# Linear attention and a gated network on one core: one list chooses the next instruction for every queue, and the first batch's norms come from products with ones

## The chip, the cores and the metric

The kernel runs on one core of a Trainium2 chip. The metric is device time in microseconds (us), from the start of one execution to its end. The five queues of the core work side by side and in order: PE (TensorE, matrix products; weight loads are shown apart as PEld), DVE (VectorE), ACT (ScalarE), POOL (GpSimd) and SP (SyncE, which here only issues transfers). An instruction that waits holds up all that stand behind it on its queue.

## The reference

Random-feature attention of 8 batches, 8 heads, 576 tokens and head dimension 64 feeds a gated network:

```
proj = x @ omega.T                   # omega 128 x 64, for q and k, scaled by 64 ** -0.25
h    = proj - sum(x * x) / 2;  phi = exp(h - max(h)) / sqrt(128)
kv   = k_p.T @ v;  z = sum over tokens of k_p
x    = (q_p @ kv) / (q_p @ z + 1e-6)         # 4608 tokens x 512
y    = sigmoid(x @ w_gate) * (x @ w_val)      # 4608 x 1536
out  = y @ w_out                              # 4608 x 512
```

Everything is float32. The network's weights come as 64-bit floats and are converted on the chip.

## The kernel before

**Stages.** The kernel has three stretches on TensorE. The first makes attention, and between its products those of the *first pass* of the network: gate and value of the first 4 of 12 column tiles of the hidden layer (tile `gv`). The second makes the other hidden columns (`gw`), the third the output (`po`). Of the first pass, 18 products are kept back and run between attention and the second stretch. The second and third stretch are written in a fixed order, which the change leaves alone; between attention and the second stretch it changes only at which products the weights `u` are loaded and split.

**Attention.** Two batches make a unit `u` (4 of them), with 9 tiles of 128 tokens and 4 pairs of heads `p`. A unit has two halves `b`; keys and queries of each half are tasks of their own, for each pair of heads (`keys` and `queries`, lines 780 to 883). A task loads its input (`rawk`, `rawq`, loaded at the top of `projected`, line 714), splits it in a high part (`hik`, `hiq`, on ACT) and a low part (`lok`, `loq`, on POOL), multiplies both with omega in three products (`ppk`, `ppq`), takes maxima on DVE, and goes on: keys to an exponential on ACT (`kpk`) and the product with v (`pkv`), queries to a subtraction (`hq`, DVE), transposes (`ptq`), an exponential (`qpq`, ACT), a product with `kv` (`pnq`), a division (`denq`, `invq`, `xq`, DVE), transposes (`pxq`), and a copy on ACT (`xsq`, 2 buffers) that goes to `xT` in memory. The first pass reads `xT` back (`xr`), splits it on ACT and POOL (`xe`) and multiplies.

**Norms.** The sums of squares come from a second copy of the input with tokens on partitions (`natk`, `natq`): for each half of a unit and of keys or queries, `norms` (line 686) loads 4 or 5 tiles of 128 x 512, squares them on ACT (`x2k`, `x2q`) and sums over each head on DVE (`ssk`, `ssq`). A task's first product with omega is not put down before its norms are.

**Weights.** `conversions` (line 284) is one long chain of 18 units `c`, each of two halves: two loads, six DVE instructions and one on POOL per half (`from_float64`, line 177), then for the first 4 units a split into `wh` and `wl`, which the first pass multiplies with, and for the others sums on POOL and a store `w32`. The load of the next unit is issued a unit ahead.

**Who orders the work.** The order of PE, DVE, ACT and POOL in attention is settled while the kernel is built. `Clock` (line 76) keeps an account of when each engine would be free and each tile written; `attention` (line 917) asks it and chooses the next step. In the kernel before, TensorE's account is "now": steps of other engines are put down while their engine is at most 2 us ahead, conversions when DVE has room, first-pass products when no attention product is due, and a hook, `filler`, slips DVE steps of conversions into attention's DVE steps. Transfers have no queue in the account: one lands 2.5 us after it could start. The account gives every float32 product 230 columns' time, and does not know TensorE's two clock levels. SP is not among the engines with an order of their own; its transfers follow the program text.

```
        if engine == "PE" and ins[0].dtype == F32:
            n = self.FULL
...
            self.written[o] = max(self.at["PE"], after, self.used.get(o, 0.0)) + self.DMA
```

Of the kernel before, what the change touches and what calls it, by code (L numbers as in the profile page):

```python
# [18 lines left out]
DM = H * D  # L19
DF = 1536  # L20
P = 128
# [27 lines left out]
LEFT = 18  # L49
SMALL = 16  # L50
SQS = 6
MARGIN = 0.5
QUEUED = 2.0
CONV_QUEUED = 0.0
CONV_LATE = 1.2
CONV_END = 0.97
CONV_FILL = 1.0
# [3 lines left out]
RAWS, SPLITS, KPS, VS, HS, XS = 6, 6, 6, 3, 4, 4  # L61
# [14 lines left out]
class Clock:  # L76
# [6 lines left out]
    DMA = 2.5  # L83
    FULL = 230

    def __init__(self):
        self.at = dict.fromkeys(self.COST, 0.0)
# [12 lines left out]
    def issue(self, engine, op, a, k):  # L100
# [9 lines left out]
        after = max(after, self.used.get(o, 0.0))  # L110
        start = max(self.at[engine], after)
# [5 lines left out]
        shared = False  # L117
        if engine == "DVE":
# [5 lines left out]
            if in_sbuf:  # L124
                shared = True
                for i, j in self.pool:
                    if i <= start < j:
                        start = j
# [4 lines left out]
        if engine == "PE" and ins[0].dtype == F32:  # L133
            n = self.FULL
        self.at[engine] = end = start + fixed + n * each
# [9 lines left out]

class Timed:
    def __init__(self, engine, name, clock):
        self.engine, self.name, self.clock = engine, name, clock
# [12 lines left out]
class Engines:  # L161
    def __init__(self, nc, clock):
        self.tensor, self.scalar, self.vector, self.gpsimd, self.sync = (
            Timed(e, n, clock)
# [12 lines left out]
def from_float64(nc, t, a, bits):  # L177
# [4 lines left out]
    yield  # L182
# [5 lines left out]
    yield  # L188
# [4 lines left out]
    yield  # L193
# [3 lines left out]
    yield  # L197

    nc.vector.tensor_scalar(out=a, in0=t, scalar1=0xFF800000, scalar2=None, op0=ALU.bitwise_and)
    yield  # L200
    r = a.bitcast(F32)
    nc.vector.scalar_tensor_tensor(out=r, in0=lo, scalar=2.0**-52, in1=r, op0=ALU.mult, op1=ALU.mult)
    yield
# [5 lines left out]
def attn_glu_kernel(ctx: ExitStack, tc, qT, kT, qn, kn, va, om, ident, w, out):  # L209
    clock = Clock()  # L210
    there = clock.there
    nc = Engines(tc.nc, clock)
# [14 lines left out]
    nc.scalar.dma_start(out=id_sb, in_=ident)  # L227
    omH = const.tile([P, 2 * M], F32R, name="omH")
# [13 lines left out]
    def bank(tag, name):  # L242
# [4 lines left out]
        if tag == "at":  # L247
# [3 lines left out]
    def release(b):  # L251
        n = clock.name(b)
        del clock.kept[n]
# [30 lines left out]
    def conversions(pool, tiles):  # L284


        ins = [j * WE for j in range(NE)] + [NE * WE + n * 4 * Q for n in range(N_LATE)]
        following = loaded(tiles("c0"), ins[0])
        for m in range(len(ins)):
            cv = following  # L290
            if m + 1 < len(ins):
                following = loaded(tiles(f"c{m + 1}"), ins[m + 1])
            if m < NE:
                ws[m] = wh, wl = [pool.tile([P, WE], F32R, name=f"{t}{m}") for t in ("wh", "wl")]
            for h in range(2):
                for _ in converted(cv, h):
                    yield "DVE", there(cv)
                yield "DVE", 0.0
                if m < NE:
                    i = slice(h * WP, (h + 1) * WP)  # L300
                    split(nc, wh[:, i], wl[:, i], cv[:, i].bitcast(F32), lo_engine=nc.gpsimd)
                    given.add((m, h))
                    yield "DVE", 0.0
            if m < NE:
                continue
            f = cv[:, : 4 * WP].bitcast(F32).rearrange("p (b q) -> p b q", q=Q)
            b, t = f[:, :4], f[:, 4:]
            for o, x, y in (
                (t[:, 0], b[:, 3], b[:, 0]),
                (t[:, 2], b[:, 2], b[:, 3]),  # L310
                (t[:, 1], b[:, 2], t[:, 0]),
                (t[:, 3], b[:, 1], t[:, 1]),
            ):
                nc.gpsimd.tensor_tensor(out=o, in0=x, in1=y, op=ALU.subtract)
                yield "POOL", 0.0
            nc.sync.dma_start(out=w32[m - NE], in_=f)

# [57 lines left out]

    def first_pass():
# [9 lines left out]

        def product(i, j, o, n, x):
            name = f"gv{o}_{j}_{i}"
            while any((j, h) not in given for h in range(2)):
                yield None  # L390
            yield "PE", max(there(*ws[j], x[0]), 0.0 if late else free_at("gv"))
# [3 lines left out]
            for k in range(KC):  # L395
                s = slice((i * KC + k) * P, (i * KC + k + 1) * P)
                xh, xl = x[k][:, 0], x[k][:, 1]
                for u, v in ((wl, xh), (wh, xl), (wh, xh)):
                    nc.tensor.matmul(gv, lhsT=u[:, s], rhs=v, start=(m == 0), stop=(m == 3 * KC - 1))
                    m += 1  # L400
                if k < KC - 1 and not late:
                    yield "PE", there(x[k + 1])
            whole[0] += 1
            return gv


        chunks = [(0, Q), (Q, Q)] + [(c * NC, NC) for c in range(1, NCH)]
# [7 lines left out]
        raw, parts = yield from begun(*chunks[0], keep)  # L415
        yield "ACT", there(raw)
        x = list(parts)
        at, homes = keep, []
        for (o, n), after in zip(chunks, chunks[1:] + [None]):
            ahead, parts, raw = [], None, None  # L420
            for j in range(NE):
                if after and parts is None and ((j == NE - 1 and ready(sum(after))) or late):

                    if late:
                        homes.append(keep if len(homes) % 2 == 0 else late)
                        at = homes[-1]
                    raw, parts = yield from begun(*after, at)
                gate = yield from product(0, j, o, n, x)
                g = keep.tile([P, 2, 2, P], F32, tag="g", bufs=2, name=f"ge{o}_{j}")
                flat = g.rearrange("p i s t -> p (i s t)")[:, :n]  # L430
# [726 lines left out]
```

## Time and profile before

| | |
|---|---|
| median of 3 runs | 1217.01 us (1212.67 to 1223.47) |
| profiled execution | 1223.85 us, of which the span of its instructions is 1222.1 us |
| busy share of the span | PE 95%, PEld 90%, DVE 71%, ACT 43%, POOL 44% |
| chain that ended last | PE 77%, DVE 7%, transfers 6%, issue 3%, ACT 3%, POOL 2% |

The busy share of PE is that of instructions in flight: a product counts as busy from its start to the end of its pipeline, and also while the clock is at its lower level. The granted clock of a stretch is given as a share of 2.4 GHz; 0.50 is the lower level, 1.2 GHz. So how much of a stretch TensorE used is better read from the number of products in it and the distance between the starts of two products that follow each other without a gap.

### The profile page before, as it was taken

What the parts mean: (1) busy time and instruction counts of PE and PEld (TensorE: products, weight loads), DVE (VectorE), ACT (ScalarE), POOL (GpSimd) and SP (SyncE); (2) the same over time, 40 slices, a digit from 0 to 9 for tenths busy, and PEclk for the clock granted to TensorE, in tenths of its full rate; (3) what the DMA queues carried; (4) which work ended last, traced back from release to release, by engine and by line L of the source; (5) the groups of instructions that cost most, each with busy time, mean ns of one, the idle gap of its engine ahead of it and who ended that gap; (6) DMA issues with size and microseconds to landing.
All of it is one profiled execution on the core that took longest, in us unless ns stands there. A gap on an engine that the chain in (4) does not pass through costs nothing.

```text
span 1222.1 us, 23996 instructions
## 1 busy us (share of the span) xinstructions
PE 1158.2 (95%) x8828; PEld 1101.3 (90%) x8828; DVE 862.2 (71%) x1917; ACT 523.5 (43%) x1176; POOL 535.4 (44%) x601
## 2 busy tenths in 40 slices
PE   3888899999999999999999999999998899999998
PEld 3777788889888988777999999999998899999998
DVE  4688978788878788743656665666568877767775
ACT  4766556555555443252422323222324543333332
POOL 1345345364654454522566666666655111101110
PEclk9799989899999999999999999999999999999999
DMA  8666548767765536374333233323337776666553
GB/s 297 198 215 199 164 139 274 230 198 235 253 212 193 192 137 212 132 271 127 136 126 126 91 126 126 126 94 123 141 140 258 218 219 190 190 190 190 190 190 113
DMA packets 104950, 219.43 MB, mean 180 GB/s; under 512 B 11136, under 2 KB 42112, under 8 KB 103040
## 3 DMA queue, kind: packets, MB, share of 16 engines
q1 hardware_dynamic: 87984, 198.94, 49.0%
q10 hardware_dynamic: 16848, 18.95, 4.4%
q8 instruction: 70, 1.15, 0.4%
q14 instruction: 48, 0.39, 0.1%
HBM read 141.82 MB, written 76.02 MB: 178 GB/s over the span
## 4 chain that ended last, share of the span: by engine, by line
PE 77%; DVE 7%; DMA 6%; issue 3%; ACT 3%; POOL 2%; SPq 1%; ACTq 0%; DVEq 0%; POOLq 0%
PE gw L154 28%; PE po L154 21%; PE gv L154 12%; PE pkv L154 4%; PE pnq L154 4%; PE ppq L154 3%; PE ppk L154 3%; DVE maxima L154 2%; PE ptq L154 2%; DVE c L154 2%; DMA xT<-xsq 1%; PE pxq L154 1%; DMA u<-w 1%; DMA natk<-kn 1%; SPq L154 1%
## 5 line engine op out<-in xcount | busy, mean ns | idle before, releaser
L154 PE MATMUL gw<-xl,u 128*128 128x256 f32 x3024 | 363.4, 283 | 5.9 <-DVE u L154 3.6
L154 PEld LDWEIGHTS gw<-xl,u 128*128 128x128 f32 x3024 | 362.4, 190 | 7.0 <-DVE u L154 4.4
L154 PE MATMUL po<-u,yh 128*128 128x256 f32 x1512 | 271.0, 282 | 0.0
L154 PEld LDWEIGHTS po<-u,yh 128*128 128x128 f32 x1512 | 233.5, 190 | 0.0
L154 PE MATMUL po<-u,yl 128*128 128x256 f32 x756 | 213.5, 282 | 3.7 <-DVE yl L154 3.7
L154 PE MATMUL gv<-xe,wh 128*128 128x512 f32 (+1 forms) x640 | 186.6, 375 | 1.8 <-DVE denq L154 0.9
L154 ACT ACTIVATE yh<-yr 128x896 fp32r<-128x896 f32 x108 | 99.2, 948 | 164.5 <-DMA yr<-yl 57.6
L154 PEld LDWEIGHTS po<-u,yl 128*128 128x128 f32 x756 | 143.5, 190 | 4.5 <-DVE yl L154 4.5
L154 POOL TENSOR_TENSOR c<-c 128x256 f32<-128x256 f32 (+1 forms) x92 | 89.1, 980 | 112.3 <-DVE c L154 54.2
L154 PEld LDWEIGHTS gv<-xe,wh 128*128 128x128 f32 x640 | 117.5, 192 | 20.9 <-POOL xe L154 4.4
L154 POOL TENSOR_TENSOR yl<-yr,yh 128x896 fp32r<-128x896 f32 x17 | 37.1, 2182 | 219.1 <-ACT yh L154 118.8
L154 POOL TENSOR_TENSOR yl<-yl,gl 128x256 f32<-128x256 f32 x106 | 96.4, 910 | 82.6 <-issue 39.2
L154 PE MATMUL gv<-xe,wl 128*128 128x512 f32 (+1 forms) x320 | 129.4, 404 | 2.2 <-ACT ge L154 0.9
L154 DVE TENSOR_TENSOR yl<-yr,yh 128x896 fp32r<-128x896 f32 x91 | 98.6, 1112 | 14.8 <-ACT yh L154 14.4
L154 DVE TENSOR_TENSOR yr<-yr 128x128 f32<-128x128 f32 x144 | 65.6, 489 | 53.9 <-DMA yr<-ye 53.4
L154 DVE TENSOR_TENSOR u<-gw,p 128x256 f32<-128x256 f32 x144 | 60.7, 421 | 58.4 <-PE gw L154 50.2
L154 POOL TENSOR_TENSOR loq<-rawq,hiq 128x256 fp32r<-128x256 f32 (+1 forms) x80 | 57.5, 729 | 72.4 <-ACT hiq L154 68.2
L154 DVE TENSOR_SCALAR c<-c 128x512 uint32<-128x512 uint32 (+1 forms) x144 | 76.7, 533 | 10.5 <-DMA c<-w 5.0
L154 PEld LDWEIGHTS pnq<-kv,qpq 128*128 128x128 f32 (+1 forms) x640 | 69.4, 184 | 11.5 <-ACT qpq L154 5.5
L154 POOL TENSOR_TENSOR lok<-rawk,hik 128x256 fp32r<-128x256 f32 (+1 forms) x80 | 56.5, 731 | 51.5 <-ACT hik L154 49.0
L154 PE MATMUL pnq<-kv,qpq 128*128 128x66 f32 (+1 forms) x640 | 73.7, 267 | 3.6 <-ACT qpq L154 2.9
L154 PE MATMUL pkv<-v,kpk 128*128 128x66 f32 x512 | 74.4, 293 | 2.1 <-ACT kpk L154 1.4
(90 smaller groups left out, 2043.7 us busy)
## 6 DMA issues: line engine op xcount, KB each, us to landing
yl<-yl SPq DMA_DIRECT2D x36, 896.0 KB, 3.6
yr<-yl SPq DMA_DIRECT2D x72, 448.0 KB, 4.1
c<-w SPq DMA_DIRECT2D x36, 512.0 KB, 4.9
xr<-xT SPq DMA_DIRECT2D x68, 256.0 KB, 3.9
w<-c SPq DMA_DIRECT2D x14, 1024.0 KB, 4.2
v<-va SPq DMA_DIRECT2D x32, 330.0 KB, 3.3
natk<-kn SPq DMA_DIRECT2D x36, 256.0 KB, 3.7
natq<-qn SPq DMA_DIRECT2D x36, 256.0 KB, 3.6
```

Of the source, the lines that this page charges most:

```text
L154: i = f(*a, **k)
```

## The change

Five things change, all but the last in the part up to the end of attention.

1. `attention` no longer goes from TensorE's "now". It makes one list of all steps that could be next (attention tasks, first-pass products, first-pass operands and gates, up to two conversion units, loads of raw inputs, stores), each with the time at which it could start by the account and a rank. The earliest start names the engine, and the best rank on that engine within 0.08 us of it is taken. An attention step on PE counts as ready 0.9 us after its inputs (0.5 before), a first-pass product 0.15 us after, a conversion step 0.2 us after unless it is behind its pace or among the first four units. The hook `filler` goes.
2. The account has a queue for SP, with its issue time and a rate for what has been sent, knows when a buffer comes free, gives float32 products of 3 to 127 columns twice the time, and slows TensorE down after stretches with little work.
3. Loads of raw inputs are steps of their own (`fetch`), in the list; the first conversion unit is loaded from 1.0 us on and the second from 12.0 us on. `xs` has three buffers for two.
4. For the first half of the first unit (`BY_PE`) there are no `norms` tasks. The task squares its own raw input on ACT, TensorE multiplies each 128 x 128 tile of the squares with a matrix of ones (two columns, one for each head), and one DVE instruction scales the result.
5. A POOL instruction waits for the last DVE instruction put down that reads two operands from SBUF, or is a wide one with a scalar (`sharing`), if none has waited for it yet. Between attention and the second stretch, weights `u` are loaded one by one, at every second product from the third on, where all five were loaded at the third.

```diff
@@ Clock.issue
-            if engine == "ACT":
-                self.at[engine] = max(self.at[engine], after) + 0.33
-            self.written[o] = max(self.at["PE"], after, self.used.get(o, 0.0)) + self.DMA
+            i = self.name(ins[0])
+            start = max(self.at[engine], self.now, after, self.used.get(o, 0.0))
+            self.at[engine] = start + self.ISSUE[engine]
+            self.sent = max(self.sent, self.at[engine]) + int(np.prod(out.shape)) * 4 / self.RATE
+            self.written[o] = self.used[i] = self.loads[o] = self.sent + self.DMA
...
-            n = self.FULL
+            n = self.FULL if n >= P else self.SHORT if n > 2 else self.FULL
@@ Timed
+            if self.name == "POOL" and self.clock.manual and self.clock.sharing:
+                self.tc.add_manual_dep(
+                    i.ins, self.clock.sharing.ins.name, mybir.DependencyInfo(mybir.DependencyClass.Sync, mybir.DependencyReason.DATA),
+                    reason="shared port",
+                )
+                self.clock.sharing = None
+            if self.name == "DVE" and self.clock.shared:
+                self.clock.sharing = i
@@ conversion (one unit, in place of the chain of all)
+        cv = tiles(f"c{m}")
+        yield "SP", BEGIN[m] if m < 2 else clock.used.get(clock.name(cv), 0.0)
+        loaded(cv, m * WE if m < NE else NE * WE + (m - NE) * 4 * Q)
...
@@ projected
-        raw = pool.tile([P, (MID + 1) * P], F32, tag="raw", bufs=RAWS, name=f"raw{name}{u}_{p}_{b}")
-        nc.sync.dma_start(out=raw[:, :n], in_=src[u, p, :, t0 * P : t1 * P])
-        while (name, u, b) not in sqs:
+        raw = raws_.pop((name, u, p, b))
+        first = (u, b) in BY_PE
+        while not first and (name, u, b) not in sqs:
             yield None
...
+            if first and not halves:
+                for i in range(0, n, 4 * P):
+                    m = min(4 * P, n - i)
+                    x2 = pool.tile([P, DM], F32, tag="x2", bufs=2, name=f"x2{name}{u}_{p}_{b}_{i}")[:, :m]
+                    nc.scalar.activation(out=x2, in_=raw[:, i : i + m], func=AF.Square)
+                    halves.append(x2)
...
+        if first:
+            yield "PE", lambda: max(there(*halves), free_at("at"))
+            ps = any_bank(f"ps{name}{u}_{p}_{b}")[:, : 2 * (t1 - t0)]
+            for i in range(t1 - t0):
+                c = i % 4 * P
+                nc.tensor.matmul(
+                    ps[:, 2 * i : 2 * i + 2], lhsT=halves[i // 4][:, c : c + P], rhs=ones, start=True, stop=True
+                )
...
@@ attention, the choice
+            first = min(ways, key=lambda x: x[:2])
+            t, _, e, a = min((x for x in ways if x[2] == first[2] and x[0] <= first[0] + TIE), key=lambda x: x[1])
+            clock.now = max(clock.now, t)
...
-            late_by = made / total < sum(through) / (NP * U * T) / CONV_END or (gate[0] is None and made < 64)
...
@@ between attention and the second stretch
-            if n == 2:
-                started = [unit(late, n) for n in range(UL)]
-                for one in started:
-                    next(one)
-            elif started and n % 3 == 0:
+            if n >= 2 and n % 2 == 0 and (n - 2) // 2 < UL:
+                started.append(unit(late, (n - 2) // 2))
+                next(started[-1])
+            if n >= 6 and n % 2 == 0 and started:
                 next(started.pop(0))
```

## Rows read from the trace of the kernel before

**Rows 1.** Busy time by stretch: stretch, length, PE, PEld, DVE, ACT, POOL, clock, transfers.

```profile
0.00:16.50 16.50, 0.00 (x0) 0.00 (x0) 5.64 (x12) 6.00 (x12) 0.97 (x6) 1.00 0.86 300
16.50:27.00 10.50, 8.02 (x39) 7.55 (x39) 7.77 (x19) 6.50 (x18) 3.17 (x5) 0.88 0.94 313
27.00:43.00 16.00, 12.94 (x60) 12.29 (x59) 7.61 (x16) 9.98 (x28) 7.54 (x10) 0.54 0.70 218
43.00:60.00 17.00, 14.14 (x95) 13.25 (x96) 13.71 (x34) 11.93 (x37) 2.81 (x4) 0.86 0.60 180
60.00:140.00 80.00, 69.42 (x555) 63.91 (x555) 70.10 (x182) 53.21 (x159) 38.13 (x48) 0.97 0.65 203
140.00:180.00 40.00, 34.97 (x248) 32.67 (x248) 31.50 (x81) 18.03 (x52) 16.26 (x19) 0.87 0.43 136
180.00:220.00 40.00, 38.25 (x291) 36.24 (x291) 27.51 (x76) 23.40 (x67) 23.99 (x30) 0.90 0.78 248
220.00:500.00 280.00, 276.10 (x1944) 247.09 (x1944) 233.10 (x600) 144.37 (x402) 142.03 (x164) 1.00 0.62 204
...
```

**Rows 2.** The same view, a stretch of 50 us inside the second stretch.

```profile
600.00:650.00 50.00, 50.00 (x422) 50.00 (x422) 30.79 (x67) 15.19 (x30) 32.05 (x39) 1.00 0.30 114
```

**Rows 3.** Timeline of PE about 305 us: start, length, engine, line, instruction, tiles.

```profile
302.41 0.40 PE L154 MATMUL gv<-xe,wl 128*128 128x512 f32 x1
...
303.10 0.39 PE L154 MATMUL gv<-xe,wl 128*128 128x512 f32 x1
...
305.54 0.33 PE L154 MATMUL pkv<-v,kmidk 128*128 128x66 f32 x2
...
307.72 0.61 PE L154 MATMUL ptq<-id_sb,hq 128*128 128x128 f32 x4
```

**Rows 4.** Timeline of all queues, first 40 us; SPq is SP issuing a transfer.

```profile
1.18 1.86 SPq L154 DMA_DIRECT2D c<-w  x4
3.08 2.20 SPq L154 DMA_DIRECT2D natk<-kn  x3
...
5.32 0.95 SPq L154 DMA_DIRECT2D rawk<-kT  x2
...
10.35 2.04 ACT L154 ACTIVATE x2k<-natk 128x512 f32<-128x512 f32 x3 [6.74 <-DMA natk<-kn]
...
15.73 3.94 POOL L154 TENSOR_TENSOR lok<-rawk,hik 128x256 fp32r<-128x256 f32 x6 [15.29 <-ACT hik L154]
...
16.52 0.58 PE L154 MATMUL ppk<-omH,lok 128*128 128x256 f32 x1 [16.52 <-POOL lok L154]
...
26.71 4.20 SPq L154 DMA_DIRECT2D natq<-qn  x2
...
31.44 0.42 SPq L154 DMA_DIRECT2D rawk<-kT  x1
...
37.37 0.58 PE L154 MATMUL ppk<-omH,lok 128*128 128x256 f32 x1 [1.61 <-POOL lok L154]
```

**Rows 5.** Transfers up to 220 us: size of one, median us from issue to landing.

```profile
rawk<-kT SPq DMA_DIRECT2D x11, 320.0 KB, 4.6
```

**Rows 6.** Groups of instructions up to 620 us: busy us, mean ns of one, idle before.

```profile
L154 PE MATMUL pkv<-v,kpk 128*128 128x66 f32 x512 | 74.4, 293 | 2.1 <-ACT kpk L154 1.4 <-ACT qpq L154 0.7
...
L154 DVE TENSOR_REDUCE ssk<-x2k 128x8 f32<-128x512 f32 x36 | 24.1, 679 | 12.6 <-ACT x2k L154 12.3
...
L154 DVE SCALAR_TENSOR_TENSOR nb<-sqk,maxima 128x10 f32<-128x10 f32 x16 | 2.7, 166 | 0.5
```

**Rows 7.** Timeline of ACT from 151 to 160 us.

```profile
155.66 0.38 ACT L154 ACTIVATE xsq<-pxq 128x256 f32<-128x256 f32 x1 [2.27 <-DMA xT<-xsq]
```

**Rows 8.** Instructions on tiles `gv`, `lok`: least/median/most ns, first and last start.

```profile
L154 PEld LDWEIGHTS gv<-xe,wl x320: 186/188/389, 90.5 to 571.6; 128*128 128x128 f32 x160
...
L154 POOL TENSOR_TENSOR lok<-rawk,hik x80: 454/738/1230, 15.7 to 421.9; 128x256 fp32r<-128x256 f32 x64, 128x128 fp32r<-128x128 f32 x16
```

**Rows 9.** Waits up to 575 us: waiter, what ended the wait, us, times, longest.

```profile
DVE maxima L154 <- PE ppk L154: 26.2, 17, 9.3
```

More of the change, by code (lines that the diff above doesn't have):

```diff
@@ L282, in attn_glu_kernel @@
     given = set()
[L284 to L292, printed above, removed]
-            if m < NE:
[L294 to L316, printed above, removed]
@@ L707, in norms @@
             )
+            if t + 3 < t1:
+                yield "SP", clock.used.get(clock.name(x), 0.0)
+                xs.append(nat(t + 3))
+        yield "DVE", there(s)
         sq = pool.tile([P, MID + 1, H], F32, tag="sq", bufs=SQS, name=f"sq{name}{u}_{b}")
@@ L920, in attention, with when @@
         active, normed = [], []
-        total, made, ended = 36 * 7 + 56, 0, False
-        wants, gate = [next(conv)], [next(gates)]
-        def fill():
-            nonlocal made
-            if wants[0] and wants[0][0] == "DVE" and wants[0][1] <= at["DVE"] + 0.1 and made / total < CONV_FILL * sum(through) / (NP * U * T) and not any(i <= at["DVE"] + 0.05 < j for i, j in clock.pool):
-                made += 1
-                wants[0] = next(conv, None)
-        filler[0] = fill
-        at = clock.at
-        n_gates = 0
-        while not ready(B * S):
+        units_, made = NE + N_LATE, 0
+        convs, gate, beside = [], [None], []
+        at = clock.at
+        def when(a):
+            return a[1]() if callable(a[1]) else a[1]
+        while not ready(B * S) or convs or made < units_ or aside or any(c[1] is not c for c in beside) or unsent:
+            while len(convs) < 2 and made < units_:
+                one = conv(made)
+                convs.append([made, one, next(one)])
+                made += 1
             while True:
@@ L957, in attention @@
                 gate[0] = next(gates)
[L959 to L962 removed]
+            ways = []
+            for a in active:
+                if a[3] is not None:
+                    ways.append((max(at[a[3][0]], when(a[3]) + MARGIN[a[3][0]]), a[0] + (LATER if a[1][0][0] == "n" else 0), a[3][0], a))
+            if gate[0] and whole[0] < 2 * NE * (NCH + 1) - LEFT:
+                e = gate[0][0]
+                ways.append((max(at[e], when(gate[0])) + (IDLE if e == "PE" else 0.0), 1000, e, gate))
@@ new lines, in attention @@
+            beside[:] = [c for c in beside if c[1] is not c] + [[c, next(c)] for c in aside]
+            del aside[:]
+            for c in beside:
+                if c[1] is None:
+                    c[1] = next(c[0])
+                if c[1] is not None:
+                    ways.append((max(at[c[1][0]], when(c[1])), ASIDE, c[1][0], c))
+            pace = sum(through) / (NP * U * T) / CONV_END * units_
+            for c in convs:
+                e = c[2][0]
+                behind = c[0] < max(pace, URGENT)
+                ways.append((max(at[e], when(c[2])) + (0.0 if behind else IDLE_DVE), (500 if behind else 2000) + c[0], e, c))
@@ new lines, in attention @@
+            if unsent:
+                ways.append((max(at["SP"], there(unsent[0][1])), 0, "SP", unsent))
+            if len(places) < RAWS or places[0] in over:
+                name = next((x for _, (x, _, _) in order[:AHEAD] if x[0][0] != "n" and x not in raws_), None)
+                if name:
+                    t = at["SP"]
+                    if len(places) == RAWS:
+                        t = max(t, clock.used.get(rawname[places[0]], 0.0))
+                    ways.append((t, 600, "SP", name))
@@ L1028, in attn_glu_kernel @@
             with tc.manual_schedule(engines={getattr(mybir.EngineType, e) for e in MANUAL}):
-                attention(pool, gates, conversions(early, tiles))
+                clock.manual = True
+                attention(pool, gates, lambda m: conversion(early, tiles, m))
+                clock.manual = False
         banks["at"] = 6
```

336 lines of the change are left out of this document (226 added, 110 removed).

## The prediction

> **What bounds the kernel now.** I read busy time by stretch first. After attention the second stretch runs 422 products in 50 us, one every 0.118 us, with PE busy all the time [rows 2]; the change leaves those products and the output's as they are, so I look only at what stands before them. For that I need the time that a product takes when the next one follows at once, from a timeline: three 512-column products of the first pass fill 0.69 us, 0.23 each, and 20 of `pkv` fill 2.18 us from 305.54 to 307.72, 0.109 each [rows 3]. Up to 180 us the first pass works on half-width operands, so nearly every product there takes 0.11 to 0.12 us; I use 0.113. Against this the number of products by stretch shows how much of TensorE was lost [rows 1]:
> - 0 to 16.5: no product; 16.5 lost.
> - 16.5 to 27: 39 products, 4.4 us of work; 6.1 lost.
> - 27 to 43: 60, 6.8; 9.2 lost. Clock 0.54, so nearly all at 1.2 GHz.
> - 43 to 60: 95, 10.7; 6.3 lost.
> - 60 to 140: 555, 62.7; 17.3 lost. DVE busy 70.10 of 80 us, 88%, the fullest engine but PE.
> - 140 to 180: 248, 28.0; 12.0 lost, clock 0.87.
> - 180 to 220: PE idle for 1.75 us; at a mean clock of 0.90 a fifth of 40 us ran at 1.2 GHz, which loses 4.0. Sum 5.8.
> - 220 to 500: idle for 3.9 us of 280, clock 1.00.
>
> So 73 us are lost before 220 us and little after. Early, TensorE waits for inputs and for DVE, and it falls to the lower clock after such waits; later it is the bound itself.
>
> Then the timeline of the first 40 us, for what ends those early waits [rows 4]. SP issues four loads of weights `c` (1.18), then three of `natk` (3.08), then raw keys (5.32). The first square of `natk` runs at 10.35 after waiting 6.74 us for its load, and the task waits for its norms: `lok` at 15.73, first product at 16.52. The second hole has the same cause: SP issues two `natq` loads over 4.20 us from 26.71, the later one waiting for a buffer, and the raw keys behind them go out only at 31.44; the product with omega follows at 37.37.
>
> **The change part by part.** The sum goes against the profiled execution, 1223.85 us (span 1222.10, 1.75 around it), which is 6.84 above the median of 1217.01.
>
> *Start.* Raw keys become the first load after omega, at about 1.2 us, with one weight unit behind the second. 320 KB take 4.6 us from issue to landing at the median [rows 5], so 5.8; after a short split on ACT the low part takes 0.74 [rows 8], and the squares and the products with ones lie beside the three low parts. First product with omega at about 8 in place of 16.52 [rows 4]: **-8.5**, between -10 and -5. The four weight loads that move back delay the conversions, which nothing needs before the first pass starts at 90.5 us [rows 8]; with that cover gone, each microsecond of delay would show there.
>
> *Loads in the list.* Raw loads no longer stand behind `nat` loads that wait for a buffer, and the first half has no `nat` loads at all: 9 of them leave SP, with their 9 waits. What is late next is POOL, which has the low parts of weights to make in the same stretch (7.54 of 16 us busy [rows 1]). Of the 9.2 us lost from 27 to 43 I take back two thirds: **-6**, between -9 and 0.
>
> *Norms by products.* Nine sums on DVE at 0.68 us [rows 6] go, 6.1 us, and eight small instructions come, at the 0.17 of `nb` [rows 6] 1.4. DVE is the fullest engine until 140 us, so this net 4.7 counts there: **-4**, and between -10 (the list also closes DVE's gaps) and 0. ACT squares as many elements as before, at no cost. TensorE gets 36 products with 2 columns. No such product is in the trace; The products of `kpk` with v, with 66, are 256 in the program (32 tasks, 2 heads, 4 tiles) and 512 instructions in the trace [rows 6], so 72 instructions come. At `pkv`'s 0.109 and the lower clock that is 15.7 us, the upper bound; wholly beside the low parts on POOL, 0. TensorE waits there anyway, so I stay near the lower one: **+2**.
>
> *Stalls from 140 to 220.* 17.8 us are lost. One cause is plain: at 155.66 `xsq` has waited 2.27 us for a store to free one of its two buffers [rows 7], and all of ACT, with the keys' exponentials, stood behind it. The third buffer removes this, and with it part of the low clock that follows. The rest is a planner that counts float32 products at half their time: `pkv` and `pnq` are 320 products each (4 units, 4 pairs of heads, 20 each), which take about 0.218 (two instructions) and were booked at half, 70 us too little over attention; so steps are put on ACT and DVE later or earlier than TensorE really wants them. With the account right I take back not quite half: **-8**, between -14 and 0.
>
> *From 220 us on.* TensorE is bound by its own products; another order can gain 3.9 us at most and can lose by putting a product ahead of its input: **0**, between -6 and +6. The weight loads one by one are counted in this.
>
> *POOL's added waits.* A POOL instruction now waits for a DVE instruction put down before it. POOL is busy 142 of 280 us from 220 to 500 [rows 1], so a short wait is covered: **0**; its price is the fourth rival's. Behind a waiting POOL instruction stand the low parts that the products with omega need.
>
> Here the trace shows both engines getting in each other's way already: `lok` takes 738 ns at the median and up to 1230 [rows 8]. The Trainium skill (SBUF — State Buffer, "Who interferes with whom") says that DVE and POOL share a pair of ports, that whoever starts first holds it for the whole instruction, and that the other is blocked. By that rule the added wait would only show what blocks POOL today, and the term would be 0 as taken; but the rule prices a DVE instruction that has started, not one that is itself waiting.
>
> Sum: -8.5 - 6 - 4 + 2 - 8 = **-24.5**, so 1199.3 for an execution like the profiled one and **1192** at the level of the median.
>
> **The rivals.**
>
> *DVE takes the gain back* (chance 0.12). TensorE starts earlier but runs into DVE, at 88% until 140 us, and its waits there grow: for is DVE's wait on products with omega (17 times, 26.2 us [rows 9]), against is DVE at 69% from 140 to 220. Then the net 4.7 us and some 4 of the stalls remain: 1208.
>
> *SP does not follow the list* (0.05). SP has no order of its own, so loads could come out in another order, and holes return; only the norms and the third buffer act: 4.7 + 2.3, so 1210.
>
> *There is more room than I think* (0.08). Between 220 and 500 us PEld is busy 247.09 of 280 us, 88% [rows 1]. The starts of the 512-column products lie 0.23 us apart [rows 3], and a load takes 0.188 of that [rows 8], so PEld cannot be full; I give this little. If room for 33 us is there and the early holes close as forecast: 1159. The Trainium skill (Perfetto Trace Analysis, "Identifying the Most-Contended Engine") judges TensorE's headroom by the busy share of weight loads, not of products; by that rule these 33 us are open.
>
> *POOL waits for a late DVE* (0.12), slower. The place is the low parts, 160 before products with omega. Where DVE is behind plan, the instruction that POOL waits for stands behind a maximum that waits for TensorE: 1.5 us a time (26.2 over 17 [rows 9]). The gain is gone when 24.5 / 1.5 = 16 such waits reach TensorE, and the kernel is over 1% slower from 24 on; at 33, 50 us are lost: 1217 - 24.5 + 50 = 1242. Against it: POOL's slack, and that DVE was ready often enough to keep TensorE at 98.6% busy from 220 to 500 [rows 1].
>
> **How the numbers follow.** The forecast, a gain between 12 and 49 us, has 0.63; its own range goes from 1168 (all lower ends, -49 after the start's, loads', norms', stalls' and late bounds: 10 + 9 + 10 + 14 + 6) to 1205. I give 1160 to 1226: it takes in the first three rivals and the weaker half of the fourth, and leaves out some 0.13. A measurement of this kernel can tell about 1%, 12 us, from no change. Faster: 0.63 + 0.08 = 0.71; within 1%: 0.12 + 0.05 = 0.17; slower 0.12.
>
> **What would show it.** First product with omega near 8 us; no stretch of 16 us at the lower clock before 60; the 997 products that had started by 180 us, by some 156; no wait of `xsq` for a store; the start of the second stretch near 548 in place of 572. Wrong: DVE over 92% with PE idle before 140, or POOL idle behind DVE with products with omega waiting for `lok` or `loq` after 220.

## The result, and the profile after

The changed kernel takes **1206.24 us** (median of 18 runs, 1203.47 to 1212.58), the kernel before beside it 1218.24: a ratio of 0.9911, 95% interval 0.9888 to 0.9933. That is faster by 12.0 us where 24.5 were forecast. The profiled execution took 1204.96 us, 18.9 below that of before; but before's lies 5.6 us above the median of its 18 runs now, and after's 1.3 below its own, so the medians carry the size and the traces say where.

Busy time by stretch of the changed kernel, as in [rows 1] and [rows 2]:

```profile
0.00:16.50 16.50, 9.07 (x50) 8.69 (x50) 7.62 (x17) 8.07 (x23) 5.31 (x11) 1.00 0.89 323
16.50:27.00 10.50, 8.30 (x39) 8.34 (x40) 9.61 (x21) 7.13 (x22) 3.21 (x3) 0.60 0.68 240
27.00:43.00 16.00, 14.78 (x81) 14.34 (x81) 8.00 (x22) 8.76 (x25) 7.31 (x10) 0.62 0.49 153
43.00:60.00 17.00, 16.82 (x121) 16.44 (x119) 14.59 (x38) 9.54 (x30) 9.40 (x11) 0.80 0.54 163
60.00:140.00 80.00, 71.12 (x553) 68.52 (x554) 66.50 (x176) 46.85 (x139) 37.16 (x45) 0.89 0.53 166
140.00:180.00 40.00, 35.53 (x259) 33.74 (x259) 33.34 (x88) 23.60 (x66) 17.90 (x25) 0.87 0.92 313
180.00:220.00 40.00, 39.16 (x300) 35.81 (x299) 36.14 (x100) 26.43 (x78) 24.80 (x29) 1.00 0.76 262
220.00:500.00 280.00, 271.31 (x1932) 241.13 (x1932) 220.67 (x580) 146.32 (x409) 136.39 (x164) 1.00 0.59 197
...
600.00:650.00 50.00, 50.00 (x431) 50.00 (x430) 31.25 (x68) 14.88 (x30) 33.85 (x41) 1.00 0.30 114
```

Three things to see. The first stretch, empty before, has 50 products. From 16.5 to 43 the clock is lower than or about as low as before (0.60 and 0.62; before 0.88 and 0.54), and from 60 to 140 it is 0.89 where it was 0.97: the same 553 to 555 products come out. And the last row, of products that the change does not touch, has 431 where there were 422.

The timeline of the first 32 us, against [rows 4]:

```profile
1.18 0.89 SPq L201 DMA_DIRECT2D rawk<-kT  x2
2.12 0.91 SPq L201 DMA_DIRECT2D c<-w  x2
...
5.67 2.30 PE L201 MATMUL psk<-ones,x2k 128*128 128x2 f32 x10 [5.67 <-ACT x2k L201]
5.88 2.67 SPq L201 DMA_DIRECT2D natk<-kn  x3
...
7.83 0.56 PE L201 MATMUL ppk<-omH,lok 128*128 128x256 f32 x1
...
11.81 0.33 SPq L201 DMA_DIRECT2D v<-va  x1
...
13.16 0.33 SPq L201 DMA_DIRECT2D v<-va  x1
...
18.70 1.95 PE L201 MATMUL pkv<-v,kpk 128*128 128x66 f32 x8 [3.41 <-DMA v<-va]
...
27.26 2.23 PE L201 MATMUL psk<-ones,x2k 128*128 128x2 f32 x10
...
31.58 0.56 PE L201 MATMUL ppk<-omH,lok 128*128 128x256 f32 x1
```

The product with omega starts at 7.83 (16.52 before). Then a new hole: two loads of `v` go out at 11.81 and 13.16, behind raw inputs, three `natk` loads and weights, and TensorE waits 3.41 us for them, to 18.70. The granted clock from there, in slices of 4 us:

```profile
14.00:18.00 4.00, 0.74 (x5) 0.42 (x3) 3.72 (x9) 3.68 (x12) 2.02 (x2) 1.00 1.03 401
...
22.00:26.00 4.00, 4.00 (x21) 4.00 (x20) 4.00 (x7) 2.22 (x7) 1.27 (x1) 0.50 0.87 294
26.00:30.00 4.00, 3.65 (x18) 3.56 (x17) 1.00 (x4) 0.83 (x2) 2.86 (x4) 0.50 0.36 101
30.00:34.00 4.00, 4.00 (x19) 4.00 (x20) 0.92 (x3) 2.66 (x7) 2.91 (x4) 0.50 0.49 124
```

While TensorE waited, the 16 transfer engines were full (share 1.03, 401 GB/s): the loads issued before had filled them. After that stretch, with 0.74 of 4 us busy, TensorE works nearly without a pause at 0.50, 1.2 GHz, up to 34 us, and many of the products with ones fall there: ten take 2.23 us. The clock column does not show all of it. In the first stretch it reads 1.00, and yet the first ten products with ones take 2.30 us, and products start 0.21 us apart up to about 11.7; in the kernel before they do so from 16.9 to 21.1. That is the distance of the lower level.

**A sum that closes.** The traces allow a cleaner account than the one of the prediction. Up to the start of the second stretch each kernel runs a fixed set of products. At the distances that they keep when they follow each other without a gap (0.2295 us with 512 columns, 0.119 for the half-width products of the first pass, 0.117 with omega, 0.098 for transposes, 0.109 else) the set is 482.1 us of work; 72 products with ones add 7.85. What is left between the first product and the second stretch is lost to gaps and the lower clock. The first `gw` product marks the end; in the tile's summary (least/median/most ns, first and last start), before and after:

```profile
L154 PE MATMUL gw<-xl,u x3024: 274/283/415, 572.5 to 943.5; 128*128 128x256 f32 x189
```

```profile
L201 PE MATMUL gw<-xl,u x3024: 274/281/387, 566.1 to 928.4; 128*128 128x256 f32 x189
```

All kernels of this case by that account (us, one profiled execution each; "rest" runs from the first `gw` to the last product; ratios to the kernel before of the same chip, with their interval):

| kernel | ratio | first product | work | lost | second stretch | rest |
|---|---|---|---|---|---|---|
| before | 1 | 16.5 | 482.1 | 73.8 | 572.5 | 644.6 |
| after | 0.9911 [0.9888, 0.9933] | 5.7 | 490.0 | 70.4 | 566.1 | 632.0 |
| e0_after_again | 0.9895 [0.9863, 0.9927] | 5.5 | 490.0 | 67.4 | 562.9 | 635.0 |
| x1_before_shift | 0.9948 [0.9921, 0.9976] | 17.9 | 482.1 | 72.8 | 572.8 | 632.8 |
| x2_after_unshift | 0.9932 [0.9906, 0.9957] | 5.8 | 490.0 | 69.2 | 564.9 | 640.9 |
| x4_apart | 0.9869 [0.9838, 0.9900] | 5.5 | 490.0 | 70.2 | 565.7 | 631.4 |
| e7_first_no_norms | 1.0028 [0.9999, 1.0057] | 5.5 | 482.1 | 79.2 | 566.8 | 647.8 |
| x3_first_no_norms | 0.9986 [0.9956, 1.0016] | 5.3 | 482.1 | 83.7 | 571.2 | 640.6 |
| e8_ones_twice | 1.0156 [1.0122, 1.0189] | 5.8 | 497.8 | 91.1 | 594.8 | 634.6 |
| e1_norms_back | 1.0052 [1.0023, 1.0082] | 19.7 | 482.1 | 74.2 | 576.0 | 637.1 |
| f1_late_start | 0.9928 [0.9905, 0.9952] | 13.3 | 490.0 | 68.2 | 571.5 | 632.5 |
| e2_no_port_wait | 0.9929 [0.9900, 0.9958] | 5.7 | 490.0 | 72.2 | 567.9 | 633.9 |
| e3_units_at_once | 0.9891 [0.9850, 0.9932] | 5.5 | 490.0 | 71.1 | 566.6 | 632.2 |
| f2_clock_off | 0.9941 [0.9916, 0.9965] | 5.6 | 490.0 | 76.8 | 572.4 | 636.1 |
| f3_short_400 | 0.9994 [0.9974, 1.0014] | 5.5 | 490.0 | 76.2 | 571.7 | 636.6 |
| e9_before_account | 1.0182 [1.0133, 1.0232] | 17.1 | 482.1 | 88.4 | 587.6 | 645.7 |
| e4_no_norms | 0.9756 [0.9715, 0.9797] | 5.5 | 482.1 | 60.4 | 548.0 | 633.6 |
| f4_best | 0.9684 [0.9659, 0.9709] | 5.4 | 482.1 | 58.9 | 546.4 | 625.9 |

Two executions of one kernel, after and e0, differ by 3 us in "lost" and by 3 in "rest", so a smaller difference between two rows says nothing. Of the 18.9 us between the profiles of before and after, 6.4 lie ahead of the second stretch and 12.6 behind it, where no instruction changed. Of these 12.6, some 8 come from products that start closer together (those less than 0.131 us apart have a mean of 119.3 ns before and 117.8 after); the other 4.6 are shorter gaps.

### The profile page after: what moved, and what is told of

Its sections match the earlier page's. It is cut to its first block, busy times and chain, and to the rows that moved or that the text cites. A ratio compares the mean times of both kernels' runs of the same rounds, so it can differ in the third digit from the quotient of the medians.

```text
span 1203.2 us, 24206 instructions
## 1 busy us (share of the span) xinstructions
PE 1157.5 (96%) x8900; PEld 1104.3 (92%) x8900; DVE 852.9 (71%) x1915; ACT 523.6 (44%) x1179; POOL 533.4 (44%) x601
## 4 chain that ended last, share of the span: by engine, by line
PE 70%; DVE 9%; DMA 4%; POOL 3%; issue 2%; ACT 1%; SPq 0%; DVEq 0%; ACTq 0%; POOLq 0%
PE gw L201 28%; PE po L201 21%; PE gv L201 10%; PE pkv L201 3%; PE pnq L201 2%; DVE maxima L201 2%; DVE c L201 2%; PE ppq L201 2%; PE ppk L201 2%; POOL c L201 2%; DMA w<-c 1%; PE ptq L201 1%; DMA u<-w 1%; DVE hq L201 1%; DMA c<-w 1%
## 5 line engine op out<-in xcount | busy, mean ns | idle before, releaser
L201 PE MATMUL gw<-xl,u 128*128 128x256 f32 x3024 | 357.6, 281 | 3.1 <-DVE u L201 2.2
L201 PEld LDWEIGHTS gw<-xl,u 128*128 128x128 f32 x3024 | 356.4, 189 | 4.3 <-DVE u L201 3.1
L201 PE MATMUL po<-u,yh 128*128 128x256 f32 x1512 | 267.9, 281 | 0.0
L201 PE MATMUL gv<-xe,wl 128*128 128x512 f32 (+1 forms) x320 | 126.2, 394 | 0.6 <-ACT ge L201 0.5
L201 DVE TENSOR_TENSOR yl<-yr,yh 128x896 fp32r<-128x896 f32 x91 | 106.7, 1198 | 17.8 <-ACT yh L201 13.9
L201 ACT ACTIVATE kpk<-ppk,nb 128x128 f32<-128x128 f32 x256 | 72.4, 385 | 39.0 <-DVE nb L201 31.7
L201 DVE TENSOR_TENSOR yr<-yr 128x128 f32<-128x128 f32 x144 | 56.7, 427 | 42.9 <-DMA yr<-ye 42.3
L201 DVE TENSOR_SCALAR c<-c 128x512 uint32<-128x512 uint32 (+1 forms) x144 | 69.4, 494 | 15.7 <-POOL c L201 13.6
L201 PE MATMUL pkv<-v,kpk 128*128 128x66 f32 x512 | 72.2, 288 | 3.4 <-DMA v<-va 3.4
```

## The experiments

**Is the rest's gain the program's?** The change runs again, unchanged.

> The changed kernel as it is, for the level of this comparison: 0.991 of the kernel before (1206 us where before takes 1218). A second profile shows whether the second and third stretch really run their products closer together than before (431 to 425 products in 50 us where before had 422), or whether that belongs to one execution: if it does, this profile will show about 422.

Measured 1204.7 us. The rest is 635.0 us, again far under 644.6, and the mean distance is 117.8 ns as in the first profile, so the closer spacing belongs to the program and not to one execution. Of the shorter gaps only 1.5 us come again.

**What moved in the program: places.** The constant `ones` has 8 bytes in a partition and takes 32, and it moves the tiles allocated behind it. I read the start addresses of the operands of each product from the compiled programs. In the kernel before, of the 5292 products of the rest, 3014 have weights and moving operand a multiple of 128 bytes apart, and 2278 are 32 or 96 off; in the change those 2278 are 64 off. Two runs move places alone.

```diff
@@ x1: kernel before, a constant that nothing uses
+    ones = const.tile([P, 2], F32, name="ones")
+    nc.vector.tensor_reduce(out=ones, in_=id_sb.rearrange("p (h d) -> p h d", d=D), axis=AX.X, op=ALU.add)
@@ x2: the change, the constant padded to 128 bytes
-    ones = const.tile([P, 2], F32, name="ones")
+    ones = const.tile([P, 32], F32, name="ones")[:, :2]
```

> The kernel before with nothing but the constant of ones added (8 bytes for each partition, one DVE instruction that fills it; nothing reads it). It moves every tile allocated after it. Theory P (places: a 256-column product takes 119.6 ns when its two operands start at the same place modulo 128 bytes, 117.8 when 32 bytes apart, 115.4 when 64 apart; the constant moved 2278 of the 5292 products after attention from 32 to 64 apart): 8 us faster than before in those stretches and some 2 in the products with omega, about 1208 of 1218, ratio 0.992. Theory O (order: the spacing belongs to single executions, the gain is the new order's): no change, 1.000.

> The changed kernel with the constant of ones widened to 128 bytes for each partition (2 of 32 columns are used), so that all tiles start at the same places modulo 128 bytes as in the kernel before; the order of all queues is unchanged. Theory P: 8 to 10 us slower than the changed kernel, 1215, ratio to before 0.997. Theory O: 1206, ratio 0.990.

Measured 1212.5 and 1210.93. An unused constant makes the kernel before some 7 us faster than its companion runs (1219.75). The products of 50 us in the second stretch, x1, then x2:

```profile
600.00:650.00 50.00, 50.00 (x432) 50.00 (x432) 32.32 (x68) 14.60 (x29) 33.30 (x41) 1.00 0.30 114
```

```profile
600.00:650.00 50.00, 50.00 (x424) 50.00 (x423) 31.99 (x69) 15.57 (x31) 32.88 (x40) 1.00 0.29 114
```

Before plus the constant has the 432 of the change, the change with the old places nearly the 422 of before [rows 2]. The order alone is worth 8 to 9 us (x2 against its companion runs), the places 3 to 7 (the change less x2; x1). That x2 is slower than the change rests on the traces, since the two intervals overlap; x1's gain stands by itself. Both runs gave less time than the 8 to 10 us that they were expected to.

All operands 64 bytes apart, with pads ahead of the tiles concerned:

```diff
-    ones = const.tile([P, 2], F32, name="ones")
+    ones = const.tile([P, 24], F32, name="ones")[:, :2]
-    omH = const.tile([P, 2 * M], F32R, name="omH")
-    omL = const.tile([P, 2 * M], F32R, name="omL")
+    om_both = const.tile([P, 4 * M + 32], F32R, name="om_both")
+    omH, omL = om_both[:, 16 : 16 + 2 * M], om_both[:, 16 + 2 * M : 16 + 4 * M]
...
+                late_u[0].tile([P, 16], F32, name="apart_l")
+        tail.tile([P, 16], F32, name="apart_t")
```

> The changed kernel with the weights u and the two omega tiles placed so that both operands of every product after attention, and of every product with omega, start 64 apart modulo 128 bytes; the order is unchanged. Theory P: 3014 products gain 4.2 ns each, 12.7 us, 1193, ratio to before 0.979; all 5292 spacings at about 115.4 ns. Theory O: 1206.

Measured 1201.45, 4 to 6 us better than the change (the intervals still overlap a little) and less than half of what was expected. The 50 us hold 434 products. In the trace the mean distance falls from 117.8 to 115.6 ns, which is 11.7 us over 5292 products and about what was foretold. But what the gaps over 0.131 us hold beyond a product's distance grows from 9 to 20 us; the waits of output products for `yl` from DVE go from 2.8 us in 3 times to 8.0 in 9. So in this execution what feeds TensorE takes the gain back.

**The norms.** First all norms back on DVE (`BY_PE = ()`, no products with ones), with the new list:

```diff
-NORMS = 6.0
-BY_PE = ((0, 0),)
+NORMS = 0.0
+BY_PE = ()
```

> The changed kernel with the norms of the first half made as in the kernel before (second copy of the input, sums on DVE), started at once. Theory A (the products with ones give the earlier start back: 72 instructions at 0.11 us, 0.21 at the lower clock, 8 to 15 us on TensorE): first product with omega at 14 to 17 us, and yet the time is within 4 us of the changed kernel, 1202 to 1210. Theory B (the products with ones lie beside other work; the gain is lost later): 7 to 10 us slower, about 1214.

Measured 1221.38, some 15 us slower than the change and outside both theories. The list without the products loses everything: its first stretch is empty again, and what is lost afterwards, 74.2 us, is that of before.

```profile
0.00:16.50 16.50, 0.00 (x0) 0.00 (x0) 8.89 (x16) 5.30 (x8) 2.79 (x6) 1.00 0.90 319
16.50:27.00 10.50, 5.44 (x29) 5.28 (x30) 10.09 (x20) 5.67 (x18) 6.99 (x8) 0.99 0.54 176
```

Then the norms of the first half left out, and the products with ones doubled:

```diff
@@ e7 and x3: a constant of zeros in place of squares and products
+    nothing = const.tile([P, MID + 1, 2], F32, name="nothing")
...
+            sq = nothing
@@ e8
-            for i in range(t1 - t0):
+            for i in [*range(t1 - t0)] * 2:
```

> Leaves out the norms of the first half (squares and products with ones; zeros stand in their place, which the subtraction of the maximum cancels). Theory A: 8 to 14 us faster than the changed kernel, about 1195. Theory B: under 4 us faster, 1203 or more.

> Each product with ones is made twice: 72 instructions more. Theory A: 8 to 13 us slower than the changed kernel, about 1216. Theory B: under 3 us slower.

Both missed. e7 came out at 1222.09, slower than the change. Its second stretch starts when the change's does (566.8), and all of the loss lies behind it: its new constant put all operands of the rest a multiple of 128 bytes apart, and 50 us hold 419 products.

```profile
600.00:650.00 50.00, 50.00 (x419) 50.00 (x419) 31.28 (x67) 14.67 (x29) 31.62 (x39) 1.00 0.29 110
```

So it was run again with `ones` padded to 96 bytes:

> As the run before that leaves out the norms of the first half, but with its constants sized so that all tiles lie where the changed kernel has them modulo 128 bytes. Theory P: the run before lost 16 us after attention to places, so this one takes about 1206, level with the changed kernel; then the norms by products cost nothing net. Theory A (they give the start back, 8 to 14 us): 1192 to 1198.

Measured 1216.37: still slower than the change, by 9 to 11 us. Of the 13.7 us between the two profiles 8.6 lie in the rest, though its operands are the same distances apart modulo 128 bytes as in the change. Ahead of it the 7.85 us of work are gone, but 83.7 are lost where the change loses 70.4.

The trace shows where. By 60 us x3 has done 30.5 us of the set of work without the ones (e7 31.4), the change 24.0, e0 26.2 and before 21.5; by 220 us x3 159.5, the change 152.8, e0 155.3. So for as long as the products with ones run, leaving them out gains 4 to 7 us. From 220 us on x3 loses 28.5 us, the change 16.7. Products of the first pass wait for their operand `xe` at two places, and at either the clock falls to 0.50 for 6.8 us (timeline of PE; the second line is busy time by stretch):

```profile
460.02 1.22 PE L201 MATMUL gv<-xe,wh 128*128 128x512 f32 x2 [2.52 <-POOL xe L201]
460.00:465.00 5.00, 4.98 (x16) 4.02 (x16) 0.00 (x0) 0.00 (x0) 5.00 (x5) 0.50 0.10 17
523.39 0.50 PE L201 MATMUL gv<-xe,wl 128*128 128x512 f32 x1 [3.57 <-ACT xe L201]
525.25 1.22 PE L201 MATMUL gv<-xe,wh 128*128 128x512 f32 x2 [1.37 <-POOL xe L201]
```

In the change the longest wait of these products for `xe` is 1.0 us from 420 us on, and the clock stays at 1.00 there. So what x3 gains early it loses late, at another place of the order.

e8 came out at 1237.06, 30 to 32 us slower than the change: its 144 products with ones, from start to next start, hold TensorE for 32.5 us where 72 took 12.8, nearly all at 1.2 GHz, and the other third of the loss lies in other gaps. So the outcome of the list answers to small edits by 10 us and more, in ways that no sum of their own durations gives.

**Where the start's lead goes.** The order of the change, with four copies of 512 KB ahead of the first keys:

```diff
+    aside_ = dram.tile([4, P, 2 * WP], U32, name="aside_")
+    for i in range(4):
+        tc.nc.sync.dma_start(
+            out=aside_[i].rearrange("p (n two) -> p n two", two=2), in_=w[:, i * WP : (i + 1) * WP, :]
+        )
```

> The changed kernel with the same order of everything, but four transfers of 512 KB (weights copied to a scratch place that nothing reads) stand on SP between omega and the first raw keys; the account does not know them. The first product with omega falls back from 7.8 us to 15 to 20 us. If the lead at the start reaches the end, as the prediction's first step has it: 7 to 12 us slower than the changed kernel, about 1215. If a later bound takes the lead back: under 3 us slower.

Measured 1211.31. The first product starts 7.6 us later than in the change and the second stretch 5.4 us later (8.6 against e0); the time is 3 to 5 us longer, each against its companion runs, between the two forecasts, and the intervals overlap. So by the traces most of a lead at the start reaches the second stretch:

```profile
L201 PE MATMUL gw<-xl,u x3024: 274/281/386, 571.5 to 934.5; 128*128 128x256 f32 x189
```

**POOL's waits and the loads one by one.**

```diff
@@ e2
-            if self.name == "POOL" and self.clock.manual and self.clock.sharing:
+            if False:
@@ e3: the five units between attention and the second stretch
+            if n == 2:
+                started = [unit(late, n) for n in range(UL)]
...
```

> The changed kernel without the added waits of POOL on DVE. Theory W (these waits give the early gain back: from 220 to 500 us products with omega wait 5.2 us in 8 gaps for low parts): 4 to 6 us faster than the changed kernel, 1201, and those 8 gaps fall to about 1 us. Rival N (the ports would have blocked POOL anyway): within 2 us, and the gaps stay.

> The changed kernel with the five weights u loaded at once after the third product and split at every third, as before. If the loads one by one are worth what the traces show after attention (gaps of more than 131 ns there add up to 17.7 us before and 12.2 to 17.4 us after): 2 to 5 us slower than the changed kernel. If they are worth nothing: within 1 us.

Measured 1211.48 and 1206.53. Without its waits the kernel is no faster, and the gaps ahead of `ppq` after 220 us, which I had laid to them, stay (4.8 us in 7; 4.6 in 7 with the waits). What ends them changes. From 220 to 500 us in the change, then without the waits:

```profile
POOL loq L201 <- DVE c L201: 13.7, 6, 5.1
PE ppq L201 <- POOL loq L201: 2.0, 3, 0.9
```

```profile
PE ppq L201 <- DVE denq L201: 1.6, 1, 1.6
PE ppq L201 <- POOL loq L201: 0.5, 1, 0.5
```

So POOL does stand behind DVE, and products with omega do wait for it, but little; without the added waits they wait for DVE as long. `lok` on POOL takes 732 ns at the median without them and 728 with them, so the waits do not shorten it either. Loads one by one are worth nothing that these runs can tell.

**The account.** The right price of float32 products in the old planner, then the new planner without its slow clock, and with a price in between:

```diff
@@ e9: kernel before
-            n = self.FULL
+            n = self.FULL if n >= P or n < 3 else 507
@@ f2
-            end = start + (end - start) * (1.85 if self.slow else 1.0)
+            end = start + (end - start)
@@ f3
-    FULL, SHORT = 230, 507
+    FULL, SHORT = 230, 400
```

> The kernel before with one line of the account changed: float32 products of 3 to 127 columns count twice, as they take. The prediction put down some of the 8 us of stalls from 140 to 220 us to this account: then 4 to 10 us faster than before, 1211. If that planner lives with its wrong account because its choices ask only what is ready: within 3 us.

> The changed kernel with TensorE's account always at full speed. If the account of the clock is part of the gain: 4 to 10 us slower, since steps up to 220 us are planned too early. If it is not: within 3 us of the changed kernel, either way.

> The changed kernel with float32 products of 3 to 127 columns counted at 400 in place of 507 (0.18 us in place of 0.224; they take about 0.218). If an account that matches what products take is worth something in this planner: 3 to 8 us slower. If the planner's result only scatters with any change of its numbers: anywhere within 8 us to either side.

Measured 1241.41, 1212.6 and 1219.03. The better account makes the old planner 20 to 22 us slower, where 4 to 10 us faster was foretold; the worse ones make the new planner 4 to 6 and 11 to 13 us slower. x3 shows that an edit which costs nothing by itself can do as much, so that the account itself is what counts is not shown. From 220 to 500 us in e9 TensorE makes 85 products fewer than in [rows 1]:

```profile
220.00:500.00 280.00, 264.50 (x1859) 235.52 (x1858) 231.95 (x583) 140.23 (x397) 143.41 (x169) 0.98 0.57 194
```

**What else bounds.** All norms left out (they cancel in what the softmax-like features use), then this with the places of x4:

```diff
-BY_PE = ((0, 0),)
+BY_PE = tuple((u, b) for u in range(4) for b in range(2))
...
-        first = (u, b) in BY_PE
...
+        first = False
```

> Leaves out all norms (they cancel when the maximum is subtracted): no second copy of the inputs, no squares, no sums, no products with ones; 48 us of work less on DVE, 46 on ACT, 7.9 on PE, 18.9 MB of loads less. If DVE and ACT bound the first 220 us, as the prediction had it: 15 to 25 us faster than the changed kernel, 1185. If TensorE's waits in attention come from the order that was chosen and from how steps depend on each other: under 8 us, the work on PE that falls away.

> All norms left out (they cancel) and the weights u and omega placed so that all products after attention, and those with omega, have their operands 64 apart modulo 128 bytes. The two changes alone took 15 and 5 us off the changed kernel; if they add: 1186 or a little less, ratio to before 0.972.

Measured 1189.49 and **1181.47**, the latter 0.9684 of before, the fastest kernel of this case. e4 from 220 to 500 us:

```profile
220.00:500.00 280.00, 274.22 (x1897) 243.44 (x1895) 194.28 (x460) 142.57 (x383) 137.12 (x158) 1.00 0.55 185
```

DVE is busy 194 us in place of 221. Ahead of the second stretch 10 us fewer are lost than in the change (7 fewer than in e0), besides the 7.85 of work. This is not where the prediction saw DVE as the bound: from 60 to 140 us e4 loses 23.3 us, more than the change (17.9); it gains from 140 to 220 (6.8 for 13.3) and after (11.1 for 16.8). So the norms' work did hold TensorE up, and late rather than early. Which part of it, that on DVE, on ACT or the loads of the second copy, no run separates.

## Why the prediction was right in direction and wrong in size

Its terms, in its order, and what the same stretch lost before and after by the account above, in the two profiles (a product counts where it starts); e0 is the second profile of the change:

| term | forecast | measured | e0 |
|---|---|---|---|
| start | -8.5 | -10.8 (16.5 to 5.7) | -11.0 |
| loads in the list, to 60 us | -6 | +0.5 (22.0 to 22.5 lost) | -1.5 |
| norms off DVE, 60 to 140 | -4 | -0.5 (18.4 to 17.9) | -1.6 |
| products with ones | +2 | +7.9 of work | +7.9 |
| stalls, 140 to 220 | -8 | -5.9 (19.2 to 13.3) | -5.2 |
| from 220 us to the second stretch | 0 | +2.5 (14.3 to 16.8) | +1.8 |
| sum ahead of the second stretch | -24.5 | -6.4 | -9.6 |
| second stretch and output | 0 | -12.6 in the profiles; 3 to 7 in time by places | -9.6 |

Part of the gain that came is luck: the 3 to 7 us by places were no part of the forecast, and without them 8 to 9 us of 24.5 are left. The prediction failed at two terms above all, the loads and the ones.

- **Start: right.** The product with omega starts at 7.83, forecast near 8, and f1 shows that most of such a lead lasts to the second stretch.
- **Loads in the list: the step that failed first.** I named POOL as what is late next. It was the transfers: with the raw inputs put early, `v` was late by 3.41 us (3.9 in e0, 7.0 in x3, which has no products with ones), and the lower clock followed. The sign foretold, no stretch of 16 us at the lower clock before 60, did not come: from 16.5 to 43 it is 0.60 and 0.62. The two thirds of 9.2 us that I took back did not come: up to 60 us as much is lost as before, and the lower clock only changed its place. Five of the 22.5 us are the ones themselves at that clock, 12.8 us taken for 7.9 of work. But x3 without them loses 24.2 up to 60. That the wait for `v` brings the lower clock is read from the order of events; f1 has no wait for `v`, loses 17.7 us up to 60, and yet has the lower clock from 27.4 for 13.7 us.
- **Products with ones: mis-sized.** I stayed near the lower end, since TensorE waits there anyway. At full clock they cost `pkv`'s price, 7.9 us, the middle of 0 to 15.7, and at 1.2 GHz twice that; they stand on TensorE's queue between products that could have run. How much of the 12.8 us that they took was hidden, x3 and e7 show: by 60 us the work done without them is 4 to 7 us more, so about half was hidden. But this price buys the start: without these products e1, which makes the norms on DVE, has neither. Start and ones together give 3.0 us by the table.
- **Norms off DVE: small.** DVE's busy time fell from 70.10 to 66.50 us between 60 and 140, but TensorE's products there did not rise (555 to 553). The sign of being wrong, DVE over 92%, did not come either (83%), and e4, with 56 us of DVE in this stretch, loses more in it: both speak against DVE as the bound there.
- **Stalls: about right in size, the reason only in part.** `xsq` waits for no store any more. What ended the idle time before it (us, times), before, then after:

```profile
  PE pxq L154: 29.8, 25
  DMA xT<-xsq: 2.9, 3
```

```profile
  PE pxq L201: 38.7, 32
  PE ppq L201: 0.5, 1
  DMA c<-w: 0.5, 1
  PE ppk L201: 0.4, 1
```

  The other half of the reason, that a right account by itself keeps steps from coming late, is not shown: in e9 it costs 20 us and more. With the new list a wrong price costs 11 to 13 us (f3), which the scatter of the list can also do.
- **From 220 us on: inside the bounds of -6 to +6.** What is lost went from 8.7 to 15.8 us up to 500, with the longest gaps ahead of `ppq` and `gv`, and from 5.6 to 0.9 after it. Attention is over earlier and more products of the first pass are left behind it.
- **"The change leaves those products as they are": wrong as a ground for costing the rest at 0.** The instructions are the same, their operands' places are not, and that is 3 to 7 us of the gain in time, which no step of the prediction foresaw.

Of the signs, then: start yes, store yes; the 997 products that are not with ones were there by 175 us, not 156 (in x3 by 159); the second stretch starts at 566.1, not 548. Of the two signs of being wrong, POOL idle behind DVE with `loq` awaited did come, for 2.0 us.

The rivals. POOL waiting for a late DVE falls: e2 without the waits gains nothing. SP not following the list falls: the loads come as listed. DVE taking the gain back is not shown: the waits at 88% that I priced did not grow, and what e4 gains beyond TensorE's own work, 7 to 10 us, comes from the work of DVE, ACT and the transfers together. More room than I think did not open: from 220 to 500 us more is lost than before (15.8 for 8.7), and PEld is at 86% of that stretch, 88 before; even in f4 the gain came from work and places taken away.

Left open: why the same list brings `xe` late in x3 and not in the change, which wait decides in e8, e9 and f3, and by which mechanism the distance of two operands acts on the spacing.

## What to carry to other kernels

A list that puts all loads first only moves the late one: ask which load is last, not only which is first. When an edit adds a constant, look where the operands of the hot products end up before believing a difference of 1%, and compare with a run that moves the places alone. A planner's account and its rule are one thing; neither can be costed by itself, and taking work away (norms that cancel) gained more than any order.

## What the runs showed of the hardware that was not expected

Spacing of products in fp32r with 256 moving columns, by the distance of the start addresses of weights and moving operand modulo 128 bytes, as means of the products of the rest that start less than 0.131 us apart, over the traces of before, x1, x2, x4, e7 and after: 119.6 to 120.0 ns at 0; 117.8 at 32; 118.2 and 119.6 at 96; 115.4 and 115.5 at 64. The distance modulo 128 does not settle it alone: in x3 the products at 64 have 117.0. With 512 columns 0 and 64 hardly differ in the change (229.5 and 229.1), but in x3 they do (229.9 and 233.3). The Trainium skill (SBUF — State Buffer, "Who interferes with whom") gives TensorE two independent read ports, one for the moving operand and one for weights, and says that it never waits on anyone. That is about other engines; between its own two reads, the 432 and 424 products in 50 us of x1 and x2 speak against independence, and the measurement decides.

A float32 product with two columns holds TensorE as long as one with 66: from start to next start 0.213 us an instruction at 1.2 GHz and 0.112 at 2.4 GHz, for `psk` as for `pkv`. Each brings the load of a weight tile on PEld, 128 x 128, longer than its own columns can explain; that the load sets the price is my reading of these rows and was not tested apart.

```profile
L201 PEld LDWEIGHTS psk<-ones,x2k x40: 186/332/338, 5.7 to 38.7; 128*128 128x128 f32 x40
L201 PE MATMUL psk<-ones,x2k x40: 207/353/374, 5.7 to 38.8; 128*128 128x2 f32 x40
```
